# Attention into a gated feed-forward on one core: the last 64 tokens laid on both halves of the partitions, contiguous weight halves, shorter warm-up products and another written-out order

## The chip, the cores and the metric

The kernel runs on one core of one Trainium2 chip. The metric is the device time of one execution in microseconds. Three executions of the kernel before are known, and one more that the hardware profiler recorded.

## The reference

For each of 8 batches and 8 heads, 576 tokens with head size 64 are condensed into 32 memories, then read back; the heads' outputs go through a two-layer network (4608 tokens, 512 to 2048 to 512):

```python
a = softmax(phi, axis=2)                       # over the 32 memories
k_m = einsum('bhsm,bhsd->bhmd', a, k); v_m = einsum('bhsm,bhsd->bhmd', a, v)
attn = softmax(q @ k_m.T / sqrt(64))           # [576, 32] per head
x = concat_heads(attn @ v_m)                   # [4608, 512]
h = x @ w_in;  g = h * clip(h + 3, 0, 6) / 6;  out = g @ w_out
```

## The kernel before, in words

The host reorders the inputs; everything else runs on the core, in fp32 precision: each large product is made of three fp32r products (high by high, low by high, high by low).

**Weights.** w_in is loaded in 8 units of two halves (`load_w1`, L176), w_out in 8 units (`load_w2`, L181). A unit is taken apart into high and low words and rounded: ScalarE (ACT) runs `magnitude` (L189) and `rounding` (L193), VectorE (DVE) `clamp` (L197), `shift` (L200), `sign` (L205) and `total` (L214); a w_out unit is then split into a high part on ACT (L221) and a low part on GpSimd (POOL, `split_low`, L225). A finished w_in unit is also written to memory (L217) and fetched back for later batches.

**Attention of one batch.** phi comes with memories on partitions (`ptile`, L247). `maxima` (L275) reduces it, `exp_phi` (L294) takes the exponential; for batches 0 and 1 TensorE (PE) turns it into token rows (`phi_turn` L313, `phi_rows` L320), for later batches a second copy with token rows is loaded (`pnat`) and `less_max` (L325) and `phi_exp` (L329) work on it. `memories` (L337) is the sum over tokens, five token tiles per batch: four of 128 tokens and one of 64 (`S - 4 * P`). Each tile is 8 products (one per head, each two instructions) into four 32-column strips of the array. Then `weights` (L348, L349), `normalise` (L354), `turn` (L359), `turned` (L363), `scores` (L370, products of 64 rows by 32 columns on both row halves), `scores_turn` (L381), `reduce` (L392), `centre` (L396), `exponent` (L399), `invert` (L403, L404), `divide` (L408), `back` (L412), `back_high` (L416), `back_low` (L421). `fold` (L435) multiplies the condensed values into w_in, so that the network's first product runs on the 32 memories per head: its result `both` is copied by `folded_high` (L446) and `folded_low` (L450).

**Network.** Work is cut into 128 slots (batch, block of 128 hidden features). In each, `gemm1` (word `g`, L466: 12 products of 288 columns) fills `ph`; `relu` (`u`, L479, ACT), `gate` (`m`, L482, DVE), `gate_rest` (`k`, L486, ACT), `high` (`h`, L490, ACT), `low` (`l`, L493, DVE) prepare `parts`; `gemm2` (`a`, L502: 12 products of 512 columns) adds four token tiles into four PSUM banks. The last 64 tokens of two batches share one tile (`Rest`, L558). `ph`, `pk`, `turns`, `pq`, `psc` and `pv` take turns in two PSUM buffers of two banks each.

**Order.** The order on every engine is written out by hand in the string ORDER: its words are played once, each issues its instructions, and each engine runs its own in that order and waits for what they need. All loads go through one queue, SP's, in the order of their words; `load_kv` (L253) takes buffers from a ring of five that w_in units 2 to 7 share, so a load waits there until its buffer is free, and the loads behind it wait too. `warm` (`wm.N`, L588) multiplies zeros by the identity into an idle bank; ORDER holds 14 of them, most in the first 50 us, `wm.7` and `wm.9` between the slots.

The words of the attention are `mx` L275, `xp` L294, `tr` L313, `pc` L320, `xa` L325, `xe` L329, `kvm` L337, `nr` L348 and L349, `nk` L354, `tp` L359, `tk` L363, `sc` L370, `ct` L381, `cm` and `ds` L392, `cs` L396, `ex` L399, `dr` L403 and L404, `dm` L408, `bt` L412, `bh` L416, `bl` L421, `fo` L435, `vh` L446, `vl` L450; of the weights `raw`, `raw2`, `ab`, `ro`, `cl`, `sh`, `si`, `to`, `sx` and `sy` in the order above, with a first number 0 for w_in and 1 for w_out. `kvm.0.4` is batch 0's fifth token tile.

Of the kernel before, what the change touches and what calls it, by code (L numbers as in the profile page):

```python
# [64 lines left out]
a.6.1 e.0.3 m.8 fo.1.3 eo.0.0 a.6.2 vh.1.3 cl.1.4 eo.0.1 h.7 h.8 si.0.4 vl.1.3 l.7 a.6.3 raw.5.0 l.8 u.9 to.0.4 m.9
g.10 a.7 h.9 k.8 raw.5.1 g.11 si.1.3 k.9 l.9 to.1.3 ab.0.5 a.8 cl.0.5 sh.1.4 u.10 m.10 ab.1.5 u.11 g.12 m.11 k.11
xa.2.2 h.10 cl.1.5 si.1.4 k.10 a.9 to.1.4 l.10 u.12 ro.0.5 sh.0.5 m.12 fo.0.3 si.0.5 a.10 h.11 g.13 h.12 l.11 raw.6.1
vh.0.3 k.12 to.0.5 sx.3 sh.1.5 a.11 u.13 l.12 m.13 fo.1.4.5 ab.0.6 vl.0.3 si.1.5 vh.1.5 sy.3 wk.3 vl.1.5 fo.0.4.5
vh.1.4 vl.1.4 raw.7.0 a.12 raw.7.1 cl.0.6 g.14 vh.0.4 h.13 wk.4 l.13 ab.0.7 a.13.0 sx.4 sh.0.6 vh.0.5 u.14 si.0.6
# [5 lines left out]
vh.1.6 g.22 si.1.7 vl.1.7 sy.6 xe.2.2 vl.1.6 h.21 l.21 kv.2.1 u.22 a.20 g.23 to.1.7 m.22 a.21 sx.7 k.22 eo.1.1 sy.7
k.20 h.22 g.24 u.23 l.22 u.24 m.23 h.23 a.22 m.24 wk.5 kv.2.3 k.23 l.23 kv.2.2 g.25 a.23.0 g.26 h.24 u.25 wk.6
fetch.2.1 e.2.0 a.23.1 wm.7 a.23.2 m.25 k.24 xe.2.0 l.24 u.26 m.26 h.26 g.27 a.23.3 kvm.2.0 kvm.2.1 kvm.2.2 kvm.2.3
kvm.2.4 a.24.0 k.25 e.2.2 a.24.1 h.25 k.26 nr.2 kv.3.3 nk.2 l.25 g.28 u.27 e.2.1 l.26 a.24.2 m.27 e.2.3 eo.2.1 g.29
u.28 m.28 h.27 a.24.3 tp.2 fetch.2.0 rc.3.0 h.28 a.25 k.28 tk.2 l.28 u.29 eo.2.0 k.27 l.27 m.29 k.29 g.30 a.26 u.30
# [5 lines left out]
ra.0.2 h.32 kv.3.0 k.33 h.33 g.35 rl.0.3 xe.3.1 l.32 a.32.0 u.34 m.34 e.3.3 xe.3.0 l.33 g.36 u.36 h.34 eo.3.1 m.36
l.34 a.32.1 k.34 u.35 ra.0.3 fetch.2.7 eo.3.0 re.0.0 m.35 re.0.1 kvm.3.0 kvm.3.1 kvm.3.2 kvm.3.3 kvm.3.4 h.35 ro2.0
g.37 h.36 a.32.2 l.35 nr.3 nk.3 kv.4.4 l.36 k.36 u.37 k.35 g.38 m.37 h.37 u.38 a.32.3 g.39 k.37 l.37 m.38 u.39 tp.3
h.38 m.39 tk.3 a.33 fo.2.4.5.6.7 vh.2.4 vh.2.5 l.38 vh.2.6 vh.2.7 vl.2.4 a.34 k.39 h.39 vl.2.5 g.40 fetch.3.2 l.39
k.38 u.40 kv.4.0 q.3.1 m.40 a.35 k.40 vl.2.7 g.41 fetch.3.3 u.41 m.41 vl.2.6 h.40 a.36 l.40 g.42 h.41 a.37 k.41 g.43
# [588 lines left out]
```

## Time and profile before

| what | us |
|---|---|
| median of three runs (lowest, highest) | 715.05 (714.21, 715.69) |
| the profiled execution: its own time | 716.04 |
| its span, first to last instruction | 714.3 |
| PE busy in the span | 691.0 |
| DVE, ACT, POOL busy | 386.8, 325.4, 79.7 |

The span is what the trace shows; 1.7 us of the profiled execution's own time lie outside it. A "busy" PE may run at either of two clock levels, which the row PEclk of the page tells by slices of the span.

### The profile page before, as it was taken

The page shows a single profiled execution, that of the slowest core. Times are in us where ns is not written, and L with a number is a line of the kernel's source. Part 1 is how long each engine was busy: PE and PEld are TensorE (multiplying, and loading weights), DVE is VectorE, ACT ScalarE, POOL GpSimd, SP SyncE. Part 2 cuts the span into 40 slices and gives each one's busy share as a digit, 9 for nine tenths or more (in the row PEclk, how much of TensorE's full clock was granted, in tenths as well). Part 3 has the DMA queues.
Part 4 walks back from the last instruction along what each step waited for, and adds up shares of the span by engine and source line. Part 5 has one row for each costly group of instructions (what it writes and reads, how often), then busy time and mean ns, then how long its engine had stood idle before and what let it go on. Part 6 is the DMA issues. An engine that isn't in the chain of part 4 may idle for free.

```text
span 714.3 us, 12530 instructions
## 1 busy us (share of the span) xinstructions
PE 691.0 (97%) x5248; PEld 576.1 (81%) x5248; DVE 386.8 (54%) x592; ACT 325.4 (46%) x635; POOL 79.7 (11%) x59
## 2 busy tenths in 40 slices
...
PEclk8589999999999999999999999999999999999999
...
GB/s 335 325 302 403 255 123 106 46 265 78 200 233 118 248 31 61 95 201 218 24 102 102 107 182 33 215 116 240 1 71 257 3 133 1 148 60 1 1 1 73
DMA packets 28247, 98.47 MB, mean 138 GB/s; under 512 B 3104, under 2 KB 3872, under 8 KB 27168
## 3 DMA queue, kind: packets, MB, share of 16 engines
...
q8 instruction: 41, 0.67, 0.4%
q14 instruction: 14, 0.11, 0.1%
...
## 4 chain that ended last, share of the span: by engine, by line
PE 88%; DVE 5%; DMA 4%; ACT 1%; issue 0%; SPq 0%; POOL 0%; POOLq 0%; DVEq 0%; ACTq 0%
PE acc L502 46%; PE ph L466 28%; PE acc L558 6%; PE pv L435 4%; PE pk L337 3%; DMA kvt<-in_kv 2%; DMA ptile<-in_pt 1%; PE psc L370 1%; DMA nmxb<-nmx 1%; DVE sm L392 1%; DVE tmp L197 1%; DMA nmx<-nmxT 1%; DVE mx L392 1%; DVE both L450 0%; DVE st L381 0%; DVE gf L482 0%
## 5 line engine op out<-in xcount | busy, mean ns | idle before, releaser
L502 PE MATMUL acc<-w,parts 128*128 128x512 f32 x1536 | 380.9, 394 | 0.0
L502 PEld LDWEIGHTS acc<-w,parts 128*128 128x128 f32 x1536 | 279.3, 188 | 63.9 <-issue 10.3
L482 DVE SCALAR_TENSOR_TENSOR gf<-gf,ph 128x576 f32<-128x576 f32 x128 | 95.6, 752 | 185.2 <-ACT gf L479 184.8
L466 PE MATMUL ph<-phi,both 128*128 128x288 f32 x1024 | 178.4, 296 | 3.5 <-DVE gf L482 1.7
L479 ACT ACTIVATE gf<-ph,three 128x576 f32<-128x576 f32 x128 | 94.7, 742 | 187.0 <-PE ph L466 159.7
L466 PEld LDWEIGHTS ph<-phi,both 128*128 128x128 f32 x1024 | 154.8, 188 | 16.1 <-DVE both L450 3.1
L493 DVE TENSOR_TENSOR parts<-gf,parts 128x512 fp32r<-128x512 f32 x128 | 91.3, 720 | 35.7 <-ACT parts L490 35.2
L466 PE MATMUL ph<-plo,both 128*128 128x288 f32 x512 | 109.0, 294 | 0.0
L490 ACT CAST parts<-gf 128x512 fp32r<-128x512 f32 x128 | 78.8, 619 | 49.7 <-DVE gf L482 21.6
L466 PEld LDWEIGHTS ph<-plo,both 128*128 128x128 f32 x512 | 82.8, 189 | 0.0
L396 POOL TENSOR_TENSOR st<-st,mx 128x576 f32<-128x576 f32 x15 | 18.6, 1252 | 412.2 <-DVE mx L392 412.2
L450 DVE TENSOR_TENSOR both<-pv,both 128x512 fp32r<-128x512 f32 x64 | 42.1, 680 | 27.0 <-ACT both L446 26.9
L446 ACT CAST both<-pv 128x512 fp32r<-128x512 f32 x64 | 35.6, 589 | 36.8 <-PE pv L435 32.4
L558 PE MATMUL acc<-w,parts 128*128 128x512 f32 x192 | 46.3, 391 | 0.0
L558 PEld LDWEIGHTS acc<-w,parts 128*128 128x128 f32 x192 | 35.6, 188 | 8.0 <-ACT o L524 0.9
L486 ACT COPY rest<-gf 128x64 f32<-128x64 f32 x128 | 30.0, 243 | 16.1 <-DVE gf L482 16.1
L435 PE MATMUL pv<-w,kvT 64*32 64x256 f32 x1024 | 33.4, 388 | 0.4 <-DVE st L381 0.4
L225 POOL TENSOR_TENSOR w<-tmp,w 128x1024 fp32r<-128x1024 f32 x8 | 20.3, 2533 | 90.2 <-ACT w L221 90.2
L435 PEld LDWEIGHTS pv<-w,kvT 64*32 64x32 f32 x1024 | 17.7, 107 | 13.3 <-issue 3.0
L337 PE MATMUL pk<-kvt,pnat 128*32 128x129 f32 (+1 forms) x640 | 24.8, 308 | 2.9 <-DMA kvt<-in_kv 2.4
L337 PEld LDWEIGHTS pk<-kvt,pnat 128*32 128x32 f32 (+1 forms) x640 | 18.9, 122 | 9.4 <-DMA kvt<-in_kv 4.2
L421 POOL TENSOR_TENSOR plo<-pT,phi 128x576 fp32r<-128x576 f32 x15 | 22.3, 1497 | 9.7 <-ACT phi L416 9.5
...
## 6 DMA issues: line engine op xcount, KB each, us to landing
...
```

The costliest lines, as they stand in the source:

```text
L337: nc.tensor.matmul(self.pk[j * M : (j + 1) * M, g, :KV], self.pnat[:rows, t, g * P + j * M : g * P + (j + 1) * M], kvt[:rows, g * NJ + j, ...
L435: nc.tensor.matmul(self.pv[u][j * M : (j + 1) * M, g], self.kvT[rows, g, j * M : (j + 1) * M], chunk[rows, j, :].bitcast(F32), start=True, ...
L446: nc.scalar.copy(both[:, 0], self.pv[u])
L450: nc.vector.tensor_tensor(both[:, 1], self.pv[u], both[:, 0].bitcast(F32), ALU.subtract)
L466: nc.tensor.matmul(self.ph[:, hf], w[:, g, fs], x[:, g * HALF : (g + 1) * HALF], start=(i == 0), stop=(i == len(seq) - 1),)
L479: nc.scalar.activation(self.halves(), self.ph, AF.Relu, bias=three)
L482: nc.vector.scalar_tensor_tensor(self.halves(), self.halves(), 6.0, self.ph, ALU.min, ALU.mult)
L486: nc.scalar.copy(rest[:, self.f, at : at + REST], self.gf[:, MAIN:])
L490: nc.scalar.copy(self.parts[:, 0], self.gf[:, :MAIN])
L493: nc.vector.tensor_tensor(self.parts[:, 1], self.gf[:, :MAIN], self.parts[:, 0].bitcast(F32), ALU.subtract)
L502: nc.tensor.matmul(accs[self.run, t], self.parts[:, k, t * P : (t + 1) * P], w, start=self.first and i == 0, stop=self.last and i == 2,)
L558: nc.tensor.matmul(accs["rest", self.p], self.parts[:, i // 2, t * P : (t + 1) * P], w2_parts(4 * self.r + t)[i % 2], start=self.r == 0 an ...
```

## The change: what it does

- `load_kv`: the 64 tokens of the fifth tile came as 64 partitions of 4128 bytes (8 heads); now group 0's four heads lie on partitions 0 to 63 and group 1's on 64 to 127, 2064 bytes each. `memories` takes its rows from the half of the group, so that the 8 products of the fifth tile stand on two row halves of the array. phi (`ptile`, `pnat`) follows: the last 64 tokens of both groups lie side by side, one turn of 128 by 128 takes the place of two of 128 by 64 (`phi_turn`), `phi_exp`, `phi_rows` work on 128 by 128 where they had 256 columns, and `less_max` becomes two instructions on 64 partitions by 128 columns.
- Weights: each half of a w_in unit, and each w_out unit, is contiguous in memory.
- `warm`: 128 columns where there were 256; 60 of them where there were 14, all ahead of slot 0.
- Homes: `both` lies 64 bytes further, in a tile 256 bytes wider; `rs` is 64 bytes wider, so that what follows it in memory moves.
- ORDER is written anew from end to end; all other words are the same ones.

```diff
 def load_kv(b, t):
-        rows = P if t < NT - 1 else S - (NT - 1) * P
-        kvt = sb.tile([P, ROW], F32, name="kvt", **KV_RING)[:, : H * KV].rearrange("p (h x) -> p h x", h=H)
-        nc.sync.dma_start(out=kvt[:rows], in_=kv[b, t, :rows])
+        heads = H if t < NT - 1 else NJ
+        kvt = sb.tile([P, ROW], F32, name="kvt", **KV_RING)[:, : heads * KV].rearrange("p (h x) -> p h x", h=heads)
+        nc.sync.dma_start(out=kvt, in_=kv[b, t] if t < NT - 1 else kl[b])
 def memories(self, t):
             for g in range(NG):
+                rows = slice(g * REST, (g + 1) * REST) if last else slice(0, P)
                 for j in range(NJ):
+                    at = t * NG * P + (0 if last else g * P) + j * M
                     nc.tensor.matmul(
                         self.pk[j * M : (j + 1) * M, g, :KV],
-                        self.pnat[:rows, t, g * P + j * M : g * P + (j + 1) * M],
-                        kvt[:rows, g * NJ + j, :],
+                        self.pnat[rows, at : at + M],
+                        kvt[rows, j if last else g * NJ + j, :],
-                        tile_position=(0, j * M),
+                        tile_position=(g * REST if last else 0, j * M),
 def less_max(self, k):
...
+            for g in range(NG):
+                rows = slice(g * REST, (g + 1) * REST)
+                nc.vector.tensor_tensor(part[rows], part[rows], self.nmx[rows, g * P : (g + 1) * P], ALU.add)
 def load_w1(u, k):
-        nc.sync.dma_start(out=part, in_=w1[u, :, k * n : (k + 1) * n])
+        nc.sync.dma_start(out=part, in_=w1[u, k])
 def load_w2(u):
-        nc.sync.dma_start(out=part, in_=w2[:, u])
+        nc.sync.dma_start(out=part, in_=w2[u])
 def weights(self):
-            self.rs = sb.tile([P, ALIGN], F32, name="rs", tag="rs", bufs=1)[:, :NG].unsqueeze(2)
+            self.rs = sb.tile([P, ALIGN + SHIFT], F32, name="rs", tag="rs", bufs=1)[:, :NG].unsqueeze(2)
 def folded_high(self, u):
-            both = vw[self.b, u] = sb.tile([P, 2, NG, UC], F32R, name="both", **VW_RING)
+            both = sb.tile([P, UNIT + ALIGN], F32R, name="both", **VW_RING)[:, SHIFT : SHIFT + UNIT]
+            both = vw[self.b, u] = both.rearrange("p (k g f) -> p k g f", k=2, g=NG)
 def warm(_):
-        nc.tensor.matmul(idle[:, :UC], ident, rest[:, :2].rearrange("p f s -> p (f s)"), start=True, stop=True)
+        nc.tensor.matmul(idle[:, :P], ident, rest[:, 0], start=True, stop=True)
 ORDER (its beginning)
-wm.1 pt.0 wm.5 raw.0.1 raw.0.0 wm.2 pt.1 wm.8 raw2.0 wm.6 raw.1.1 wm.3 raw.1.0 wm.12 kv.0.2 kv.0.0 mx.0 kv.0.1 xp.0.2
-xp.0.1 tr.0.2 wm.11 ab.0.0 kv.0.3 xp.0.0 cl.0.0 kv.0.4 ro.0.0 tr.0.0 mx.1 tr.0.1 sh.0.0 xp.1.1 si.0.0 xp.1.0 q.0.1
-ab.1.0 to.0.0 q.0.0 pc.0.0 pc.0.2 pc.0.1 cl.1.0 raw2.1 xp.1.2 sh.1.0 tr.1.0 ab.0.1 si.1.0 tr.1.1 ro.1.0 cl.0.1 sh.0.1
-ro.0.1 kvm.0.0 to.1.0 pc.1.0 kv.1.0 kvm.0.1 si.0.1 sx.0 kvm.0.2 kv.1.2 sy.0 kvm.0.3 kv.1.1 kvm.0.4 kv.1.3 wm.0 nr.0
-kv.1.4 nk.0 q.1.0 to.0.1 tp.0 tk.0 pc.1.1 sc.0.1 sc.0.0 ct.0.1 cm.0.1 fo.0.1 ct.0.0 vh.0.1 cs.0.1 ab.1.1 cm.0.0 fo.0.0
-cs.0.0 ex.0.1 wm.13 cl.1.1 vh.0.0 ds.0.1 ex.0.0 ro.1.1 sh.1.1 dr.0.1 vl.0.0 dm.0.1 ds.0.0 tr.1.2 kvm.1.0 dr.0.0 bt.0.1
-kvm.1.1 raw.2.0 dm.0.0 kvm.1.2 raw.2.1 bh.0.1 q.1.1 kvm.1.3 bt.0.0 pc.1.2 bl.0.1 raw2.2 kvm.1.4 vl.0.1 raw.3.0 bh.0.0
-wm.10 pt.2 nr.1 bl.0.0 nk.1 raw2.5 raw2.3 si.1.1 tp.1 g.0 raw.4.1 tk.1 to.1.1 ab.0.2 raw.6.0 sc.1.0 u.0 wm.4 cl.0.2
-ro.0.2 m.0 ct.1.0 g.1 h.0 sh.0.2 l.0 sc.1.1 cm.1.0 u.1 a.0.0 ct.1.1 k.0 ab.1.2 cs.1.0 a.0.1 m.1 g.2 si.0.2 h.1 ex.1.0
-ro.1.2 cm.1.1 fo.1.1 to.0.2 a.0.2 vh.1.1 k.1 u.2 a.0.3 cs.1.1 vl.1.1 raw.3.1 wk.1 m.2 g.3 raw2.6 l.1 ex.1.1 pn.2 sx.1
-cl.1.2 raw.4.0 fo.0.2 wk.2 sh.1.2 u.3 a.1 ds.1.0 sy.1 raw2.4 h.2 dr.1.0 vh.0.2 m.3 ro.1.5 vl.0.2 ds.1.1 dm.1.0 ab.1.3
-g.4 ro.1.3 l.2 si.1.2 a.2 h.3 k.2 u.4 to.1.2 ab.0.3 dr.1.1 l.3 k.3 g.5 sx.2 dm.1.1 m.4 bt.1.0 ro.0.3 sy.2 a.3 bt.1.1
-u.5 h.4 m.5 k.4 bh.1.1 l.4 bh.1.0 fo.1.0 bl.1.1 mx.2 fo.1.2 a.4 vh.1.2 q.2.1 bl.1.0 q.2.0 vh.1.0 mo.2 vl.1.2 h.5
...
+wm.48 wm.14 pt.0 wm.30 raw2.1 wm.18 pt.1 wm.45 raw.0.0 wm.5 wm.16 raw.0.1 wm.26 wm.49 raw2.0 wm.43 wm.27 raw.1.0 wm.34
+wm.54 raw.1.1 wm.59 wm.29 wm.13 wm.19 kv.0.0 mx.0 wm.10 wm.47 wm.7 wm.44 wm.41 wm.51 wm.20 xp.0.1 wm.53 wm.55 xp.0.0
+xp.0.2 kv.0.1 tr.0.0 ab.1.1 wm.17 wm.37 wm.21 wm.31 ro.1.1 wm.38 kv.0.2 mx.1 wm.57 wm.9 wm.28 tr.0.2 wm.3 wm.0 wm.11
+cl.1.1 kv.0.3 xp.1.1 wm.42 wm.52 sh.1.1 wm.33 xp.1.0 tr.0.1 wm.58 si.1.1 ab.0.0 kv.0.4 wm.35 to.1.1 ro.0.0 cl.0.0
+pc.0.0 q.0.1 ro.1.0 sh.0.0 si.0.0 pc.0.1 pc.0.2 ab.1.0 tr.1.0 to.0.0 wm.2 tr.1.1 xp.1.2 ab.0.1 cl.1.0 wm.32 sh.1.0
+kvm.0.0 pc.1.0 si.1.0 ro.0.1 wm.36 kv.1.1 kvm.0.1 cl.0.1 q.0.0 pc.1.1 sh.0.1 kv.1.0 kvm.0.2 to.1.0 wm.25 kv.1.2
+kvm.0.3 kvm.0.4 kv.1.3 wm.24 nr.0 kv.1.4 wm.22 si.0.1 wm.56 nk.0 q.1.1 wm.46 tp.0 to.0.1 tk.0 sc.0.1 fo.0.0 ct.0.1
+wm.40 vh.0.0 cm.0.1 sc.0.0 vl.0.0 cs.0.1 ct.0.0 tr.1.2 kvm.1.0 pc.1.2 cm.0.0 ex.0.1 fo.0.1 raw.2.0 cs.0.0 kvm.1.1
+q.1.0 ds.0.1 kvm.1.2 ex.0.0 raw.2.1 dr.0.1 vh.0.1 kvm.1.3 raw.5.0 ds.0.0 wk.0 dm.0.1 kvm.1.4 raw2.2 wm.6 dr.0.0 wm.50
+nr.1 raw.3.1 wm.39 nk.1 bt.0.1 wm.12 wk.1 tp.1 dm.0.0 bh.0.1 wm.8 bt.0.0 tk.1 bl.0.1 raw2.3 sc.1.1 vl.0.1 bh.0.0 wm.23
+ct.1.1 sx.0 wm.4 raw.3.0 wm.15 wm.1 bl.0.0 sc.1.0 sy.0 g.0 ct.1.0 ab.0.2 raw2.7 cm.1.0 cm.1.1 g.1 u.0 cl.0.2 ro.0.2
+cs.1.1 m.0 g.2 u.1 cs.1.0 h.0 m.1 ex.1.1 l.0 g.3 h.1 sh.0.2 k.0 ex.1.0 l.1 u.2 a.0.0 si.0.2 sx.1 a.0.1 to.0.2 k.1 u.3
+a.0.2 ab.1.2 m.3 sy.1 a.0.3 raw.5.1 wk.2 m.2 fo.0.2 pt.2 ds.1.1 h.2 fo.1.2 q.2.0 a.1 vh.0.2 pn.2 dr.1.1 l.2 raw2.5
+ab.1.3 raw.4.0 dm.1.1 ds.1.0 k.3 ab.0.3 vl.0.2 cl.1.2 k.2 g.4 sh.1.2 vh.1.2 ro.1.2 dr.1.0 si.1.2 a.2 u.4 dm.1.0 vl.1.2
...
```

## Rows read from the trace of the kernel before

**Rows 1.** The page, part 2: the granted clock of PE in 40 slices.

```profile
PEclk8589999999999999999999999999999999999999
```

**Rows 2.** Busy us of each engine (instructions), clock, DMA share and GB/s, by stretch.

```profile
0.00:62.04 62.04, 44.28 (x409) 28.44 (x409) 44.82 (x69) 38.68 (x68) 12.97 (x14) 0.78 0.93 334
62.04:126.00 63.96, 63.96 (x455) 53.34 (x456) 59.15 (x87) 46.80 (x88) 15.18 (x8) 1.00 0.54 192
```

**Rows 3.** Waits of PE from 64 to 709: engine, line, waited for, us, times, longest.

```profile
PE ph L466 <- DVE both L450: 0.4, 1, 0.4
```

**Rows 4.** The longest waits of DVE up to 64 us; columns as in rows 3.

```profile
DVE rs L348 <- PE pk L337: 6.0, 2, 4.3
DVE tmp L197 <- ACT tmp L189: 3.5, 1, 3.5
DVE nmx L275 <- DMA ptile<-in_pt: 3.4, 1, 3.4
```

**Rows 5.** Timeline of DVE: start, us, line, operation, idle before it.

```profile
11.88 0.68 DVE L200 TENSOR_SCALAR tmp<-tmp 128x1024 uint32<-128x1024 uint32 x1
12.60 1.29 DVE L205 SCALAR_TENSOR_TENSOR tmp<-raw,tmp 128x512 uint32<-128x512 uint32 x2
13.81 1.29 DVE L214 CUSTOM_DVE_ANT_0 w<-raw,tmp 128x1024 uint16<-128x1024 uint16 x2
15.01 0.69 DVE L197 TENSOR_SCALAR tmp<-tmp 128x1024 f32<-128x1024 f32 x1
...
25.63 0.16 DVE L348 TENSOR_SCALAR rs<-pk 128x2 f32<-128x2 f32 x1 [4.25 <-PE pk L337]
...
29.23 0.78 DVE L381 STREAM_TRANSPOSE st<-psc 128x576 f32<-128x576 f32 x1 [2.05 <-PE psc L370]
...
52.45 2.25 DVE L214 CUSTOM_DVE_ANT_0 w<-raw,tmp 128x1024 uint16<-128x1024 uint16 x2
...
56.49 2.88 DVE L197 TENSOR_SCALAR tmp<-tmp 128x1024 f32<-128x1024 f32 x1
```

**Rows 6.** Timeline of PE: batch 1's `memories` and the fifth `gemm1`.

```profile
36.49 3.67 PE L337 MATMUL pk<-kvt,pnat 128*32 128x129 f32 x64
...
62.04 1.04 PE L466 MATMUL ph<-phi,both 128*128 128x288 f32 x4 [1.29 <-DVE gf L482]
```

**Rows 7.** Stretches of 1.6 us; columns as in rows 2.

```profile
17.60:19.20 1.60, 1.36 (x18) 0.59 (x16) 1.57 (x4) 1.60 (x3) 0.00 (x0) 0.50 1.09 403
19.20:20.80 1.60, 0.49 (x12) 0.39 (x12) 1.60 (x3) 1.60 (x4) 0.00 (x0) 0.50 1.05 177
20.80:22.40 1.60, 1.55 (x32) 1.00 (x23) 0.57 (x1) 0.46 (x1) 1.06 (x1) 0.50 0.98 230
...
32.00:33.60 1.60, 1.60 (x18) 0.50 (x2) 1.57 (x4) 1.60 (x3) 0.04 (x1) 0.50 1.08 184
...
36.80:38.40 1.60, 1.60 (x36) 1.47 (x32) 1.57 (x4) 0.67 (x1) 0.00 (x0) 0.50 0.14 42
```

**Rows 8.** Timeline of POOL: the first `split_low`.

```profile
21.34 2.35 POOL L225 TENSOR_TENSOR w<-tmp,w 128x1024 fp32r<-128x1024 f32 x1 [20.04 <-ACT w L221]
```

**Rows 9.** The chain that ended last, in order: start, us, what.

```profile
277.12 1.89 PE pv L435 x64
...
392.32 1.58 PE ph L466 x12
...
394.61 2.47 PE pk L337 x80
```

**Rows 10.** Timeline of PE around `wm.7`.

```profile
164.66 0.85 PE L502 MATMUL acc<-w,parts 128*128 128x512 f32 x3
165.36 0.59 PE L588 MATMUL acc<-rest,ident 128*128 128x256 f32 x2
165.60 1.05 PE L502 MATMUL acc<-w,parts 128*128 128x512 f32 x3
166.49 0.68 PE L466 MATMUL ph<-phi,both 128*128 128x288 f32 x4
```

More of the change, by code (lines that the diff above doesn't have):

```diff
@@ L65 @@
[L65 to L69, printed above, removed]
@@ L75 @@
[L75 to L79, printed above, removed]
@@ L85 @@
[L85 to L89, printed above, removed]
@@ new lines @@
+ab.1.3 raw.4.0 dm.1.1 ds.1.0 k.3 ab.0.3 vl.0.2 cl.1.2 k.2 g.4 sh.1.2 vh.1.2 ro.1.2 dr.1.0 si.1.2 a.2 u.4 dm.1.0 vl.1.2
+h.3 fetch.2.2 m.4 ro.1.3 to.1.2 k.4 h.4 g.5 l.3 sx.2 l.4 bt.1.1 sy.2 a.3 u.5 bt.1.0 ro.1.7 m.5 bh.1.1 mx.2 bh.1.0
+bl.1.1 fo.1.1 fo.1.0 vh.1.1 mo.2 a.4 vh.1.0 bl.1.0 vl.1.1 raw2.4 h.5 vl.1.0 ab.1.5 l.5 k.5 cl.1.3 sp.2 ro.1.5 q.2.1
+g.6 cl.0.3 raw2.6 ro.0.3 sh.0.3 sh.1.3 a.5.0 u.6 si.0.3 g.7 ro.0.5 m.6 si.1.3 k.6 a.5.1 h.6 u.7 g.8 l.6 e.0.0 m.7
+a.5.2 to.0.3 u.8 a.5.3 e.0.1 m.8 eo.0.0 a.6.0 h.7 e.0.3 raw.4.1 ro.1.4 g.9 to.1.3 e.0.2 cl.1.5 k.7 eo.0.1 k.8 a.6.1
```

235 lines of the change are left out of this document (126 added, 109 removed).

## The prediction

> **What bounds the kernel now.** I read the stages first. Up to 62.04 us, where the fifth `gemm1` (`g.4`) begins, PE is busy 44.28 us at a mean clock of 0.78; in the next 63.96 us it is never idle [rows 2], and between 64 and 709 us it waits 0.4 us in all [rows 3]. So from slot 4 on the time is PE's own work, at full clock [rows 1]; nothing that another engine does there is worth anything, and what is left to gain is the start and the number and size of PE's products. Then I asked what holds the start. `g.4` waits 1.29 us for `gate` on DVE [rows 6], and DVE is busy 44.82 of the 62.04 us [rows 2], so the start is a queue of DVE work with holes of 17.2 us in it. The holes: 3.4 us for the first phi, 3.5 for the first weights, 6.0 in two waits for `memories` (4.25 ahead of `nr.0`, so 1.75 ahead of `nr.1`) [rows 4, 5], 2.05 ahead of `ct.0.1` [rows 5]. Behind them stand the loads: DMA moves 403 GB/s, and 177 and 230 while the 64-row tile `kv.0.4` is under way, 184 for `kv.1.4` [rows 7].
>
> **The start.** I compare DVE's work ahead of `g.4` in the two orders. Before, DVE must reach `m.3`; after, `vl.0.2`, which frees the PSUM buffer. Both lists have 54 words; they differ in four (`dr.1.0 vl.1.1 cl.1.2 sh.1.2` against `vl.0.2 ds.1.1 dr.1.1 l.2`), a reciprocal pair, a `vl` and two operations of 0.7 us on either side. PE's products ahead of `g.4` differ only in which unit is folded. So `g.4` moves by what DVE's holes shrink or grow.
>
> *Hole for the second phi.* `raw2.1` now comes ahead of `pt.1` in place of `raw.0`'s two halves, the same bytes, so I let `pt.1` land as before. DVE has no `cl.0.0` (0.69 [rows 5]) to do while it waits: 3.5 + 0.69 = 4.2 us where 3.5 were, 0.7 worse. Contiguous rows may make it land sooner; the floor is no wait.
>
> *Hole ahead of `nr.0`.* After `mx.1`, at about 11.9 us, the new order holds `cl`, `sh`, `si`, `to` of `raw2.1` and `raw.0`, then `cl sh si` of `raw2.0`, `cl.0.1 sh.0.1`, `to.1.0`. From start to start one `sh` takes 0.72, `si` 1.21, `to` 1.20, `cl` about 0.7 [rows 5]; four `cl`, four `sh`, three `si`, three `to` are 2.8 + 2.9 + 3.6 + 3.6 = 12.9, so DVE works until 24.8. `kvm.0.4`, which ends the wait, comes with its load. Ahead of that load's end stand 1.05 MB more than before (`raw2.1`), 2.6 us at 403 GB/s [rows 7]. The half-partition load cost (2 x 403 - 177 - 230) x 1.6 / 403 = 1.6 us [rows 7]; on 128 partitions I let it go at the common rate. So 2.6 - 1.6 = 1.0 later, less some 0.4 for fewer rounds in PE (below): `nr.0` at 26.2 against 25.63, and a hole of 1.4 against 4.25. The bound on the other side: the load is as slow on 128 partitions, and `nr.0` comes at 27.8.
>
> The Trainium skill, SBUF — State Buffer, section "Door 1: The DMA port swizzle (why [64,N] ≈ [32,N])", says that partitions 0 to 63 reach only half of the 16 DMA ports and measures 196 against 328 GB/s. By it, as an estimate, 264 KB would gain 0.5 us and not 1.6, and the gain below would be 1.1 us smaller; the trace's rates (half, over two stretches) bear the larger figure, so I keep it.
>
> *Hole ahead of `ct.0.1`.* It came 3.6 us after `nr.0` [rows 5], so at 29.8; `nr.0`, `si.0.1` and `to.0.1` fill 0.35 + 2.4 of them: 0.85 against 2.05.
>
> *Hole ahead of `nr.1`.* Ahead of it stand `ct.0.1 cm.0.1 vl.0.0 ct.0.0 cm.0.0 cs.0.0 ds.0.1 dr.0.1 ds.0.0 dr.0.0`, eight of 0.7 and two of 0.45, 6.5 us, so 36.3. The same bytes as before lie ahead of `kv.1.4`; the queue had run dry by 36.8 to 38.4 (42 GB/s [rows 7]), and two half-partition loads give back 3.2, so it lands by about 35 and `kvm.1.4` is done: hole 0 against 1.75. `vl.0.0` stands early, so batch 1's `pk` gets its buffer some 4 us sooner, and `raw.2.0`, which waits for a kv buffer, is issued before the queue runs dry.
>
> *The small holes*, 17.2 less 3.4 and the 11.55 just named, are 2.3 us in all. I keep them, with one new among them: `m.1` waits for `u.1` behind `ro.0.2` on ACT.
>
> Before: 3.5 + 4.25 + 2.05 + 1.75 = 11.55. After: 4.2 + 1.4 + 0.85 + 0 = 6.45. **Start: 5.1 us sooner.** Bounds: DVE also lost 2.2 us in one `cl` (2.88 against 0.69) and 1.0 in a pair of `to` (2.25 against 1.29) [rows 5], both beside work on POOL; should that go, 8.3. With the loads no faster 1.6 and, at `nr.1`, about 0.7 go: 2.8. `sy.0` (2.35 us [rows 8]) ran in the hole ahead of `nr.0` and now runs behind `sx.0`, about 40 us, where DVE is dense: if `cl.0.2` waits as the long `cl` did, another 2.2 go: 0.6.
>
> **Zeros.** One `wm` of 256 columns costs PE 0.43 us at full clock: from 165.36 to 166.49 is 1.13, three products of 512 alone 0.70 [rows 10]. `wm.7` and `wm.9` no longer stand between the slots: **0.9 us**. One of 128 columns is 0.22 at full and 0.43 at half clock; 26 stand ahead of the first `tr`, where PE waits for phi, 34 behind it, 14.6 us at half clock against 17.8 us of idle PE [rows 2]. Where they cover nothing they delay: four ahead of `tp.0` and four of `tp.1` may each cost 0.6. This is in the bounds, with -0.6 in place of 0.6.
>
> **Fifth tile.** `memories` is 80 instructions in 2.47 us, four strips at a time: 20 rounds of 0.12. The fold, on 64 rows by 32 columns, does 64 of twice the columns in 1.89 [rows 9], which is eight rounds of eight at 0.24: both row halves at once. So the last 16 take two rounds in place of four: 0.25 a batch, six batches behind slot 4, **1.5 us** (0 if the halves don't overlap). Two `less_max` on 64 partitions for one, `phi_exp` on half the columns and one `tr` for two lie on DVE, ACT and an idle PE: nothing, while DVE keeps up.
>
> **Homes.** Twelve products of `gemm1` take 1.58 us [rows 9], and the 128 such sets read `both` at six homes; I take 0, and 0.01 a set, 1.3 us, to either side.
>
> **Sum.** 716.04 - 5.1 - 1.5 - 0.9 = 708.5 for the profiled execution; it stood 1.0 above the median, so **707.5** for the median. What a measurement tells from no change is about 0.2%, 1.4 us.
>
> **Rivals.**
>
> *The loads hold it.* The fifth tile is no faster and the 1.05 MB counts in full: the start gives 2.8 and not 5.1: 715.05 - 2.8 - 2.4 = 709.9. For it: DMA's share is 0.93 all through the start [rows 2]. Chance 0.16.
>
> *The port.* `sy.0` meets `cl.0.2` on the memory port that the long `cl` seems to have waited for, 2.2 us [rows 5], and the start gives 2.9: 709.8. Against it: `cl.0.2` may come after its end. Chance 0.10. The Trainium skill, SBUF — State Buffer, section "SBUF: two separate sides", calls the port pair that DVE and GpSimd share an exclusive lock, the loser blocked for a whole instruction; the `cl` of 2.88 us, four times its like, agrees.
>
> *Given back.* Behind slot 4 DVE is busy 59.15 of 63.96 us [rows 2]. If the new order makes PE wait there for DVE by the start's 5.1 us, only 2.4 remain: 712.7. Against it: as much DVE work is done at `g.4` as before. Chance 0.12.
>
> *The clock, and slower.* From 17.6 to 38.4 us every stretch shows the granted clock at 0.50, 1.2 of 2.4 GHz, also where PE was busy 1.60 of 1.60 us [rows 7]; full clock is back only behind 3.67 us of dense products on 128 rows [rows 6, 1]. The new order cuts these apart (`fo.0.1` between `kvm.1.0` and `kvm.1.1`) and leans on zeros. If these fail, `g.0` to `g.3` run at half clock, 4 x 1.58, and `a.0` and `a.1` add 2 x 2.8 (four times 0.70 each [rows 10]): 11.9 - 7.5 = 4.4 slower, 719.5. It decides from where it costs 7.5, that is, if the clock is still low in `a.0`. Against it: the first slice stands at 8 tenths [rows 1], so zeros alone had raised it. Chance 0.14.
>
> **Chances.** The forecast, from 704.5 to 709, has 0.48. Faster: 0.48 + 0.16 + 0.10 + 0.03 of those given back = 0.77; same: 0.09 of those and 0.02 of the clock's = 0.11; slower 0.12. The range reaches from 703 (start 8.3, `pt.1` sooner by 1.5) to 715, where the clock's case begins.
>
> **What would show it.** DVE's wait ahead of `nr.0` near 1.4, none ahead of `nr.1`, `g.4` at about 57; no stretch at 200 GB/s at the fifth tiles; the 80 instructions of `memories` in 2.2 us; PE without waits behind `g.4`. Wrong it would be with PEclk at 0.5 beyond 45 us, a `cl.0.2` of over 2 us, or PE waits for DVE between 60 and 130 us.

## The result, and the profile after

| | before | after |
|---|---|---|
| median (lowest, highest), us | 714.63 (713.28, 715.69), 4 runs | 707.25 (706.76, 708.52), 4 runs |
| span of the profiled execution | 714.3 | 705.5 |
| `g.4` begins, slot 64, slot 112 | 62.04, 376.00, 624.57 | 56.14, 368.60, 616.02 |

The ratio is 0.9896, 95% interval 0.9875 to 0.9916: faster, by 7.4 us. Of the span's 8.8 us, 5.9 are won up to `g.4` and 2.9 behind it. Line numbers of after are a little higher: `total` is L217, `memories` L348, `weights` L359, `fold` L446, `gemm1` L478, `gate` L494, `gemm2` L514, `split_low` L228.

DVE's timeline of after, which answers to [rows 5] (last column: idle before, and what ended it):

```profile
8.65 1.35 DVE L279 TENSOR_REDUCE nmx<-ptile 128x2 f32<-128x1152 f32 x1 [2.56 <-DMA ptile<-in_pt]
...
23.87 0.16 DVE L359 TENSOR_SCALAR rs<-pk 128x2 f32<-128x2 f32 x1 [0.98 <-PE pk L348]
...
26.62 0.78 DVE L392 STREAM_TRANSPOSE st<-psc 128x576 f32<-128x576 f32 x1
...
33.78 0.10 DVE L359 TENSOR_SCALAR rs<-pk 128x2 f32<-128x2 f32 x1
...
40.58 0.68 DVE L200 TENSOR_SCALAR tmp<-tmp 128x1024 f32<-128x1024 f32 x1
...
46.28 3.47 DVE L217 CUSTOM_DVE_ANT_0 w<-raw,tmp 128x1024 uint16<-128x1024 uint16 x2
49.67 1.41 DVE L494 SCALAR_TENSOR_TENSOR gf<-gf,ph 128x576 f32<-128x576 f32 x2
...
53.37 0.68 DVE L462 TENSOR_TENSOR both<-pv,both 128x512 fp32r<-128x512 f32 x1
```

The four holes that the prediction added up (4.2, 1.4, 0.85 and 0) are 2.56, 0.98, 0 and 0. But `to.0.2` at 46.28 takes 3.47 us where a pair took 1.29 [rows 5]. POOL's timeline shows what ran beside it, `sy.1` (`sy.0`, at 37.94, ends before `cl.0.2`). I call it a meeting when operations of DVE and POOL run side by side and one of them takes far longer than alone:

```profile
37.94 2.44 POOL L228 TENSOR_TENSOR w<-tmp,w 128x1024 fp32r<-128x1024 f32 x1 [0.99 <-ACT w L224]
...
46.55 2.65 POOL L228 TENSOR_TENSOR w<-tmp,w 128x1024 fp32r<-128x1024 f32 x1 [3.15 <-ACT w L224]
```

And PE's timeline, for `a.0`, two folds, `a.1` and `g.4`, shows what that cost:

```profile
45.21 2.93 PE L514 MATMUL acc<-w,parts 128*128 128x512 f32 x12
50.47 1.58 PE L446 MATMUL pv<-w,kvT 64*32 64x256 f32 x32 [2.33 <-DVE gf L494]
51.98 4.33 PE L514 MATMUL acc<-w,parts 128*128 128x512 f32 x12
56.14 0.68 PE L478 MATMUL ph<-phi,both 128*128 128x288 f32 x4
```

PE waits 2.33 us for `gate`, which stands behind `to.0.2` on DVE, and twelve products like those that took 2.93 then take 4.33. `vl.0.2`, the last line of DVE above, ends at 54.05; `g.4`, which the prediction let wait for it, comes 2.1 us later, behind `a.1`. By stretch (columns as in [rows 2], the clock third from the end) DMA moves 414 and 415 GB/s while `kv.0.4` lands and 321 at `kv.1.4`, where [rows 7] had 177 and 230, and 184; the clock is full all through, but for the stretch behind PE's wait, where it falls to 0.50:

```profile
20.80:22.40 1.60, 1.05 (x18) 0.68 (x18) 1.56 (x3) 0.64 (x2) 0.00 (x0) 1.00 1.05 414
22.40:24.00 1.60, 1.35 (x35) 0.87 (x35) 0.62 (x2) 0.00 (x0) 0.00 (x0) 1.00 1.03 415
...
30.40:32.00 1.60, 1.60 (x56) 1.12 (x56) 1.53 (x4) 1.17 (x3) 0.00 (x0) 1.00 1.02 321
...
52.00:54.00 2.00, 2.00 (x9) 1.61 (x6) 2.00 (x5) 2.00 (x5) 1.41 (x1) 0.50 1.04 422
54.00:56.00 2.00, 2.00 (x9) 1.59 (x8) 1.93 (x6) 2.00 (x4) 0.09 (x1) 0.79 1.01 407
...
62.00:126.00 64.00, 62.76 (x453) 52.63 (x452) 58.55 (x86) 49.23 (x87) 12.61 (x6) 1.00 0.49 169
```

Behind 62 us PE, which waited 0.4 us there before [rows 3], now waits 2.9 us in all:

```profile
PE ph L478 <- DVE both L462: 1.2, 4, 0.5
PE pv L446 <- DMA w<-w_kept: 0.9, 1, 0.9
PE ph L478 <- DVE gf L494: 0.8, 1, 0.8
```

The 96 instructions of the fifth tile in the six batches behind the start keep PE busy 2.7 us, where before it was 3.9 (line, shape, count, busy us and mean ns):

```profile
L348 PE MATMUL pk<-kvt,pnat 64*32 64x129 f32 x96 | 2.7, 282 | 0.0
```

One more difference was in no step of the prediction. From start to start, by place in the twelve and as a median over the slots between 130 and 640 us, `gemm2`'s first four products took 235, 231, 232, 231 ns before and 226, 227, 227, 227 after.

### The profile page after: what moved, and what is told of

It is laid out like the page before. It is cut to its first block, busy times and chain, and to the rows that moved or that the text cites. A ratio compares the mean times of both kernels' runs of the same rounds, so it can differ in the third digit from the quotient of the medians.

```text
span 705.5 us, 12734 instructions
## 1 busy us (share of the span) xinstructions
PE 687.3 (97%) x5338; PEld 581.0 (82%) x5338; DVE 384.2 (54%) x598; ACT 325.3 (46%) x635; POOL 79.6 (11%) x59
## 5 line engine op out<-in xcount | busy, mean ns | idle before, releaser
L514 PE MATMUL acc<-w,parts 128*128 128x512 f32 x1536 | 378.9, 393 | 0.0
L514 PEld LDWEIGHTS acc<-w,parts 128*128 128x128 f32 x1536 | 280.8, 189 | 61.4 <-issue 6.5
L494 DVE SCALAR_TENSOR_TENSOR gf<-gf,ph 128x576 f32<-128x576 f32 x128 | 95.5, 752 | 177.2 <-ACT gf L491 177.0
L478 PE MATMUL ph<-phi,both 128*128 128x288 f32 x1024 | 175.9, 294 | 2.4 <-DVE both L462 1.2
L478 PEld LDWEIGHTS ph<-phi,both 128*128 128x128 f32 x1024 | 154.6, 188 | 14.4 <-issue 3.0
L505 DVE TENSOR_TENSOR parts<-gf,parts 128x512 fp32r<-128x512 f32 x128 | 87.6, 692 | 41.1 <-ACT parts L502 40.5
L478 PE MATMUL ph<-plo,both 128*128 128x288 f32 x512 | 109.9, 296 | 0.0
L478 PEld LDWEIGHTS ph<-plo,both 128*128 128x128 f32 x512 | 81.6, 188 | 0.1
L446 PE MATMUL pv<-w,kvT 64*32 64x256 f32 x1024 | 32.7, 382 | 3.3 <-DVE gf L494 2.3
L446 PEld LDWEIGHTS pv<-w,kvT 64*32 64x32 f32 x1024 | 17.9, 106 | 15.2 <-DVE gf L494 3.9
L228 POOL TENSOR_TENSOR w<-tmp,w 128x1024 fp32r<-128x1024 f32 x8 | 19.7, 2464 | 77.0 <-ACT w L224 77.0
L410 ACT ACTIVATE st<-st 128x576 f32<-128x576 f32 x16 | 10.9, 685 | 25.9 <-POOL st L407 25.5
L348 PE MATMUL pk<-kvt,pnat 128*32 128x129 f32 (+1 forms) x640 | 19.9, 277 | 2.0 <-DMA kvt<-in_kv 1.9
```

Source lines behind the costliest of these rows:

```text
L446: nc.tensor.matmul(self.pv[u][j * M : (j + 1) * M, g], self.kvT[rows, g, j * M : (j + 1) * M], chunk[rows, j, :].bitcast(F32), start=True, ...
L478: nc.tensor.matmul(self.ph[:, hf], w[:, g, fs], x[:, g * HALF : (g + 1) * HALF], start=(i == 0), stop=(i == len(seq) - 1),)
L494: nc.vector.scalar_tensor_tensor(self.halves(), self.halves(), 6.0, self.ph, ALU.min, ALU.mult)
L505: nc.vector.tensor_tensor(self.parts[:, 1], self.gf[:, :MAIN], self.parts[:, 0].bitcast(F32), ALU.subtract)
L514: nc.tensor.matmul(accs[self.run, t], self.parts[:, k, t * P : (t + 1) * P], w, start=self.first and i == 0, stop=self.last and i == 2,)
```

## Experiments

Ratios are to the kernel before, run on the same chip in the same rounds (its medians there 715.62, 714.53 and 714.64 us). The changed kernel itself, run again, gives 0.9899.

### What the loads are worth

**The old fifth tile** (64 rows by 8 heads, 16 products in four strips) in the changed kernel:

```diff
-        nc.sync.dma_start(out=kvt, in_=kv[b, t] if t < NT - 1 else kl[b])
+        nc.sync.dma_start(out=kvt[:rows], in_=kv[b, t, :rows])
-            tile_position=(g * REST if last else 0, j * M),
+            tile_position=(0, j * M),
... (and the layout of phi and of the rows that goes with it)
```

> The changed kernel with the old form of the last 64 tokens: 64 rows by 8 heads in one load, phi's two transposes, 16 products in four strips. The prediction's two steps together (theory): each of the two loads 1.6 us later, a hole of some 2.5 us ahead of `nr.0` in place of 0.98, and four rounds in place of two in each of eight batches, 1.2 behind the start: 707.25 + 1.6 + 0.4 + 1.2 = 710.5. If the load on half the partitions is hidden (rival): only the rounds, 708.5, with the wait ahead of `nr.0` still near 1 us.

Measured 712.13 us (708.45 to 713.23), ratio 0.9941 [0.9918, 0.9963]. `kv.0.4` lands at 24.88 us where after has 23.27: the load is worth 1.61, and the hole ahead of `nr.0` is 3.19 in place of 0.98. The first theory holds (the ratio is 3 us above that of the changed kernel run again), with a surprise in the profiled execution, the lowest of six, 708.45: `g.0` begins 3.6 us later than after's, `g.4` 0.14 earlier. DVE, then POOL:

```profile
26.08 0.16 DVE L351 TENSOR_SCALAR rs<-pk 128x2 f32<-128x2 f32 x1 [3.19 <-PE pk L340]
...
49.88 1.29 DVE L217 CUSTOM_DVE_ANT_0 w<-raw,tmp 128x1024 uint16<-128x1024 uint16 x2
```

```profile
50.15 3.27 POOL L228 TENSOR_TENSOR w<-tmp,w 128x1024 fp32r<-128x1024 f32 x1 [3.16 <-ACT w L224]
```

`sy.1` begins 0.27 us behind `to.0.2`, as in after, but here it is POOL that waits (3.27 against some 2.4) and DVE that goes through. Who wins is not fixed by the order of the words.

**Weights in pieces of rows**, as before, in the changed kernel:

```diff
-        nc.sync.dma_start(out=part, in_=w1[u, k])
+        nc.sync.dma_start(out=part, in_=w1[u, :, k * n : (k + 1) * n])
-        nc.sync.dma_start(out=part, in_=w2[u])
+        nc.sync.dma_start(out=part, in_=w2[:, u])
... (and the host's arrays)
```

> The changed kernel with the weights' halves as before, pieces of rows of a larger array in place of contiguous blocks. If contiguous halves made the second phi land sooner (theory; it landed at 8.53 us and before at 10.49, behind as many bytes): `pt.1` lands at 9.5 to 10.5, DVE's wait for it is 3.5 to 4.5 us in place of 2.56, and the time is 1 to 2 us more, 708.5 to 709. If the new order of the first loads alone did that (rival): the wait stays at 2.6 and the time at 707.3.

Ratio 0.9903 [0.9886, 0.9920], 707.74 us: no difference that can be measured. For the second phi and the time the rival was right: the wait is 2.81 us, nearly as after. But further on, which neither guess looked at, `kv.0.4` lands at 24.37, 1.10 later than in after, and `nr.0` comes at 25.32, 1.45 later (PE's clock stood at 0.50 from 22 to 24 us, in after at 1.00, so not all of the 1.45 need be the load's). Contiguous weights do speed the loads; `g.4` begins at 56.08 all the same, because PE's clock did not fall behind its wait in this execution:

```profile
51.93 1.33 PE L446 MATMUL pv<-w,kvT 64*32 64x256 f32 x32 [2.33 <-DVE gf L494]
53.19 3.06 PE L514 MATMUL acc<-w,parts 128*128 128x512 f32 x12
```

### What the order and the zeros are worth

**The old order**, with its 14 products of zeros of 256 columns, all else as after:

```diff
 ORDER (its beginning)
-wm.48 wm.14 pt.0 wm.30 raw2.1 wm.18 pt.1 wm.45 raw.0.0 wm.5 wm.16 raw.0.1 ...
+wm.1 pt.0 wm.5 raw.0.1 raw.0.0 wm.2 pt.1 wm.8 raw2.0 wm.6 raw.1.1 wm.3 ...
-        nc.tensor.matmul(idle[:, :P], ident, rest[:, 0], start=True, stop=True)
+        nc.tensor.matmul(idle[:, :UC], ident, rest[:, :2].rearrange("p f s -> p (f s)"), start=True, stop=True)
```

> The order of before, with its 14 products of zeros of 256 columns, on the changed loads, fifth tile, weights and homes. If loads and homes carry the gain (theory): the wait ahead of `nr.0` falls from 4.25 us to about 2.5 and that ahead of `nr.1` from 1.75 to 0, so the start is 3.4 us sooner, the fifth tile is worth 1.2 behind it and the homes 3.5 to 4: 706 to 706.5, so the new order with its zeros is worth nothing net. If the order carries the pitch and the most of the start (rival): 3.4 and 1.2 alone, 710.

706.18 us, ratio 0.9866 [0.9847, 0.9885]: at the least not slower than after. The time is the first theory's. `nr.0` comes at 20.75, behind a wait of 0.45 where I expected 2.5 (before 4.25 [rows 5]), `nr.1` behind 1.54; `g.4` at 56.90. In DVE's and PE's timelines:

```profile
20.75 0.16 DVE L356 TENSOR_SCALAR rs<-pk 128x2 f32<-128x2 f32 x1 [0.45 <-PE pk L345]
...
51.35 2.89 DVE L197 TENSOR_SCALAR tmp<-tmp 128x1024 f32<-128x1024 f32 x1
```

```profile
56.90 1.04 PE L475 MATMUL ph<-phi,both 128*128 128x288 f32 x4 [1.28 <-DVE gf L491]
```

The first theory had the wait ahead of `nr.0` too long, since it counted the tile alone: `kv.0.4` lands at 20.15 us, 4.28 sooner than before, of which the tile's form is worth some 1.6, and the second phi at 9.29 where it was 10.48. The rest is the contiguous weights'. So the changed loads and homes alone bring `g.4` 5.14 us forward. The new order is worth 0.8 more there, which it gives back: behind 62 us the old one has one wait of 0.6 where the new one has 2.9.

**No zeros at all** (60 words taken out of ORDER):

```diff
-wm.48 wm.14 pt.0 wm.30 raw2.1 wm.18 pt.1 ...
+pt.0 raw2.1 pt.1 ...
```

> The changed kernel without any of its 60 products of zeros (their output is read by nobody). If the zeros hold TensorE's clock up (theory, the prediction's rival on the clock): the granted clock is 0.5 from some point of the start until the dense products, `g.0` to `g.3` take up to twice their 0.79 us a half and `a.0`, `a.1` up to twice 2.8: 5 to 11 us later, 712 to 718. If the true products alone keep the clock, the zeros only stand in PE's way (rival): the same to 1 us faster, 706 to 707.

706.42 us, ratio 0.9868 [0.9849, 0.9886]: not slower than with them. The clock is lower in two stretches of the start,

```profile
24.00:36.00 12.00, 8.27 (x164) 3.40 (x163) 11.19 (x21) 4.89 (x11) 3.41 (x3) 0.80 1.02 382
36.00:46.00 10.00, 9.98 (x73) 8.59 (x66) 7.67 (x13) 7.75 (x14) 5.84 (x4) 0.73 1.00 406
```

but `g.4` begins only 0.65 us later. The time is the rival's, and the mechanism in part the theory's: in these two profiles the zeros hold the clock, and a lower clock there costs little. They don't hold it always: in the profile of the changed kernel run again, zeros and all, it falls to 0.56 between 22 and 24 us and to 0.59 between 36 and 40. And something speaks for leaving them out: without them `kv.0.4` lands at 22.05 us, 1.22 sooner than in after, and `nr.0` comes without a wait. The other pair of runs below shows the same (22.03 against 23.15); why, no run shows.

### The meeting on the memory

**The changed kernel again**, for its spread:

> The changed kernel unaltered, for the same chip as the other three: 707 to 708.5 (0.9896 of before). If `to.0.2` meets `sy.1` in every execution its runs lie within 1 us of each other; if the meeting turns on a tenth of a microsecond (the run with the old fifth tile missed it by 0.27 us in its profile and had runs from 708.4 to 713.2), some lie 3 us lower.

707.80 us (703.95 to 708.82), ratio 0.9899 [0.9877, 0.9921]; one of six runs lies 2.6 us below the next. In its profile (span 706.9) `to.0.2` met `sy.1`, and before that `bl.0.0`, 0.71 us alone, met `sy.0`:

```profile
38.94 2.92 DVE L432 TENSOR_TENSOR plo<-pT,phi 128x576 fp32r<-128x576 f32 x1
...
49.61 3.47 DVE L217 CUSTOM_DVE_ANT_0 w<-raw,tmp 128x1024 uint16<-128x1024 uint16 x2
```

My expectation said of the run with the old fifth tile that it missed the meeting; its rows above show that it met and won.

**`sy` earlier**:

```diff
-... tk.0 sc.0.1 fo.0.0 ct.0.1 wm.40 vh.0.0 cm.0.1 sc.0.0 vl.0.0 cs.0.1 ct.0.0 ... sx.0 ... sy.0 ... sx.1 ... sy.1
+... tk.0 sc.0.1 fo.0.0 ct.0.1 wm.40 vh.0.0 sx.0 cm.0.1 sc.0.0 vl.0.0 cs.0.1 sy.0 ct.0.0 ... sx.1 ... sy.1
```

> The changed kernel with four words moved: `sx.0` behind `vh.0.0` and `sy.0` behind `cs.0.1` (POOL is idle there from 29.4 to 32.4 us), and `sx.1 sy.1` at the old places of `sx.0 sy.0`, so that no `sy` runs beside `to.0.2`. If the meeting of `sy.1` and `to.0.2` on the memory costs the start its 2.2 us and, through PE's idle time of 2.33 us and the clock that falls behind it, another 1.4 to 1.6 (theory): `to.0.2` takes 1.28 us in place of 3.47, `a.1` 2.8 in place of 4.33, `g.4` begins at 52.5 us in place of 56.1, and the time is 703.5 to 704. If something else ends last there, the loads or POOL (rival): `g.4` at 55 or later, 706 to 707.3.

706.67 us, ratio 0.9889 [0.9874, 0.9903]; `g.4` at 55.92. `to.0.2` takes 1.29, as expected, but the moved `sy.0` meets another operation, `cs.0.0`, alone 0.76. DVE, then POOL:

```profile
30.99 2.08 DVE L406 TENSOR_TENSOR st<-st,mx 128x576 f32<-128x576 f32 x1
```

```profile
30.08 2.38 POOL L227 TENSOR_TENSOR w<-tmp,w 128x1024 fp32r<-128x1024 f32 x1
```

The meeting was moved, not removed. `cs.0.0` stands ahead of `nr.1` on DVE, which comes at 35.80 in place of 33.78, and `g.0` begins 3.1 us later than in after.

**`sy.1` later**, by one word:

```diff
-... si.0.2 sx.1 a.0.1 to.0.2 k.1 u.3 a.0.2 ab.1.2 m.3 sy.1 ...
+... si.0.2 a.0.1 to.0.2 k.1 u.3 a.0.2 ab.1.2 sx.1 m.3 sy.1 ...
```

> The changed kernel with one word moved: `sx.1` behind `u.3` and `ab.1.2` on ACT, so that `sy.1`, which waits for it, begins at 48.4 us, after `to.0.2`, and runs beside `m.3 m.2 ds.1.1`, of which none was slowed beside POOL so far; `l.2` and the small add of `dr.1.1` may wait for its end at 51. If the meeting with `to.0.2` is what the start loses (theory): `to.0.2` 1.28 us, PE's wait of 2.33 us gone, no clock drop, `g.4` at 52.5 to 53 and 704 us on this scale (before at 714.5 to 715.6). If behind slot 4 DVE can't follow (the prediction's rival, given back): `g.4` as soon, but PE's waits behind it grow from 2.9 us to 5 or more, and the time is 706 to 707.

706.18 us (704.48 to 707.80), ratio 0.9869 [0.9848, 0.9890]; the profiled execution, one of 704.48, spans 702.7. DVE, POOL, PE, and PE's waits behind 36 us:

```profile
46.17 1.28 DVE L216 CUSTOM_DVE_ANT_0 w<-raw,tmp 128x1024 uint16<-128x1024 uint16 x2
47.37 1.41 DVE L493 SCALAR_TENSOR_TENSOR gf<-gf,ph 128x576 f32<-128x576 f32 x2
48.70 0.75 DVE L402 TENSOR_REDUCE sm<-st 128x18 f32<-128x576 f32 x1
49.48 1.33 DVE L413 TENSOR_SCALAR sm<-sm 128x18 f32<-128x18 f32 x1
```

```profile
48.38 2.40 POOL L227 TENSOR_TENSOR w<-tmp,w 128x1024 fp32r<-128x1024 f32 x1 [5.09 <-ACT w L223]
```

```profile
49.43 3.04 PE L513 MATMUL acc<-w,parts 128*128 128x512 f32 x12
52.96 0.79 PE L477 MATMUL ph<-phi,both 128*128 128x288 f32 x4 [0.49 <-DVE both L461]
```

```profile
PE ph L477 <- DVE both L461: 1.7, 5, 0.5
PE ph L477 <- DVE gf L493: 1.1, 2, 0.8
PE pv L445 <- DMA w<-w_kept: 0.7, 1, 0.7
```

This is the theory's picture: `to.0.2` at its own length, no wait of 2.33 us, `a.1` at full clock, `g.4` 3.18 us sooner, and of these 2.81 are still there at the last slot. Only a small add, 0.18 alone, now waits out `sy.1` (1.33). The rival, given back, takes 0.4. The timed runs stand only some 2 us below after's, where the theory had 3, on intervals that overlap. The mean granted clock of each execution tells a part of the rest: the two at 704.5 us have 1.000 and 0.999, the three longer ones 0.994 to 0.998, so in these the clock fell somewhere. That after often misses its meeting is not borne out: in all eight traced executions with `sy.1` at after's place (after's, the same kernel again, the old fifth tile, the weights in rows, no zeros, and three with old homes) it begins beside `to.0.2`. DVE lost in seven of them, POOL in one, and behind the seven waits of PE, of 2.29 to 2.44 us, the clock fell in five. How these cases are spread over the executions without a trace is not known.

**That, and no zeros**:

```diff
-... si.0.2 sx.1 a.0.1 ... ab.1.2 m.3 sy.1 ...   (and 60 words wm.N)
+... si.0.2 a.0.1 ... ab.1.2 sx.1 m.3 sy.1 ...
```

> The run with `sx.1` later, and without the 60 products of zeros (nobody reads their output). If the zeros are worth a clock step where PE idles in the start (theory, from the run without zeros alone: `g.4` 0.65 us later): `g.4` some 0.6 to 1 us later than in the run with them, 704.6 to 705. If they are worth nothing or stand in the way (rival): the same within 0.3 us, or sooner.

705.14 us, ratio 0.9860 [0.9843, 0.9877]. In the profile `g.4` comes 0.71 later than with the zeros (53.67), as the theory says; in the timed runs nothing is lost. In two pairs, then, the zeros gain 0.7 us at `g.4` in a profile and no time that can be measured.

### The homes

Four combinations of old and new homes, all else as after:

```diff
-            both = sb.tile([P, UNIT + ALIGN], F32R, name="both", **VW_RING)[:, SHIFT : SHIFT + UNIT]
-            both = vw[self.b, u] = both.rearrange("p (k g f) -> p k g f", k=2, g=NG)
+            both = vw[self.b, u] = sb.tile([P, 2, NG, UC], F32R, name="both", **VW_RING)
-            self.rs = sb.tile([P, ALIGN + SHIFT], F32, name="rs", tag="rs", bufs=1)[:, :NG].unsqueeze(2)
+            self.rs = sb.tile([P, ALIGN], F32, name="rs", tag="rs", bufs=1)[:, :NG].unsqueeze(2)
```

Both edits:

> The changed kernel with the old homes of `both` and `rs` (no 64 columns more, no shift of 16), everything else as after (707.25). If the homes set the pitch of the products (theory): the first four products of each `gemm2` go back from 227 ns to 231 to 235 and `gemm1` loses some 10 ns a slot, together 3.5 to 4 us over 128 slots: about 711, with the start unchanged (the fifth `gemm1` at 56.1 us). If the new order sets the pitch and the homes are worth nothing, as the prediction had it (rival): 707.3 and a pitch of 227 ns.

Only the second:

> The changed kernel with the old home of `rs` (64 columns, so all tiles behind it lie 64 bytes lower), and the new one of `both`. If `both`'s own 64 bytes set the pitch of `gemm1` alone and the tiles behind `rs` that of `gemm2` (theory): `gemm1` as after (126 and 128 ns at its second and third product), `gemm2`'s first four products back at 231 to 235 ns, 2 us slower than after. If `both` sets the two (rival): all as after, 707.3; if the tiles behind `rs` set the two: 2.5 to 3 slower.

Only the first:

> The changed kernel with the old home and size of `both`, and the new one of `rs`, the fourth of four combinations. With the two old the products lost 1.45 ns each in `gemm2` and 0.65 in `gemm1`, with `rs` alone old more. If the distance between `both` and the tiles that are read with it decides (theory): as bad as the other mixed one, a last slot 4 us later than after's, 711. If the home of the tiles behind `rs` decides alone (rival): as after, 707.3, with 227 ns at `gemm2`'s first products.

Start to start in ns (medians as above), and how much later than after's the last slot begins, counted from `g.4`:

| `both`, `rs` | `gemm2`, products 1 to 4 | `gemm1`, 2, 3, 10 | last slot, us | time, ratio |
|---|---|---|---|---|
| new, new (after) | 226, 227, 227, 227 | 126, 128, 131 | 0 | 707.80, 0.9899 |
| old, old | 235, 231, 232, 231 | 133, 132, 140 | 2.5 | 710.29, 0.9918 [0.9898, 0.9938] |
| new, old | 233, 236, 226, 231 | 132, 132, 132 | 4.1 | 711.01, 0.9946 [0.9926, 0.9966] |
| old, new | 237, 233, 236, 225 | 140, 132, 132 | 5.4 | 714.96 (one run) |

The old order on the new homes shows after's pitch (226, 227, 227, 227), so the order has no part in it. Neither home decides alone: the two mixed ones are the worst. The pitch and the last slot are read from one trace each. In the timed runs the two old homes cost 1.4 us, by ratios whose intervals (0.9898 to 0.9938, and 0.9877 to 0.9921 for the changed kernel again) still overlap; with only `rs` old it is 3.4, clear of the noise. That is against what I expected of the run with the old `rs` (`both`'s own home leaves `gemm1` as slow as the old one), and with the first theory of the last run, by more than it said. In the last row's one run `g.4` also comes 2.1 us later than in after, which is in its time and not in the column before it.

### A version that beats both

The old order on the changed loads and homes, two words moved behind `l.2` and the two products of zeros between the slots left out:

```diff
-... pn.2 sx.1 cl.1.2 raw.4.0 fo.0.2 wk.2 sh.1.2 u.3 ... g.4 ro.1.3 l.2 si.1.2 a.2 ...  wm.7 ... wm.9
+... pn.2 sx.1 raw.4.0 fo.0.2 wk.2 u.3 ... g.4 ro.1.3 l.2 cl.1.2 sh.1.2 si.1.2 a.2 ...
```

> The old order on the changed loads and homes, with `cl.1.2 sh.1.2` moved behind `l.2`, so that no `cl` of 2.89 us stands ahead of `m.3`, for which PE waits 1.28 us, and without `wm.7` and `wm.9`, 0.43 us each between the slots. If these are what that order loses (theory): `g.4` at 55.6 us in place of 56.9 and 0.86 us less behind it, 704 to 704.4 where the old order alone gave 706.2. If another operation takes the `cl`'s place beside `sy.1`, or `si.1.2` comes too late behind it (rival): 705 to 706.

703.13 us (702.10 to 703.52), ratio 0.9828 [0.9810, 0.9846]: 4.9 us under the changed kernel by the ratios, on intervals that don't touch, and below the 704 of the theory. In place of the `cl` of 2.89, the small add waits for `sy.1`, and `g.4` no longer waits for `gate`:

```profile
51.75 1.60 DVE L411 TENSOR_SCALAR sm<-sm 128x18 f32<-128x18 f32 x1
```

```profile
55.11 0.68 PE L475 MATMUL ph<-phi,both 128*128 128x288 f32 x4
```

## Why the prediction was right

The number was right, 707.5 for 707.25, and so was the mechanism at large: a start shorter by its loads, and fewer products behind it. Its parts were off in both directions, and that the errors cancelled so closely is luck. Between the two profiled executions 8.8 us were won where the parts add up to 7.5; the median agrees to 0.25 because the one before stood 1.0 above its median and that of after stands at its own.

- **Half-partition load: right.** 1.6 us was the price; 1.61 is what `kv.0.4` lands sooner than in the run with the old form, and 2.2 at `nr.0`, with the rounds, where 2.0 were counted (the clock stood at 0.50 there in that run from 24.0 to 25.6 us, and at 1.00 in after). By the two rates that the Trainium skill, SBUF — State Buffer, section "Door 1: The DMA port swizzle (why [64,N] ≈ [32,N])", measures for half and for all partitions, the prediction had 0.5 as an estimate; the run bears three times that.
- **Contiguous weights: priced at nothing.** The prediction let `pt.1` land as before and the loads behind it go at the old rate. They are worth 1.1 us at `kv.0.4` and up to 1.45 at `nr.0`. The second phi is another matter: it lands 1.95 us sooner with a w_out unit ahead of it, and 1.84 with that unit in pieces (the wait is 2.56 and 2.81), where the prediction had let it land as before. With the two, DVE's holes fell from 11.55 to 3.5 us and not to 6.45.
- **The port: right in kind, wrong in place.** `sy.0` did not meet `cl.0.2`; `sy.1` met `to.0.2`, 2.2 us, and with PE's idle time and the clock behind it the meeting cost 3.2 at `g.4`, which the profile of the run with `sy.1` later shows. This pair stood in no rival, and its cost is about the 2.9 that the two gains left out above had won. The Trainium skill, SBUF — State Buffer, section "Who interferes with whom", says that a DVE instruction with two inputs in SBUF contends with a GpSimd instruction that reads SBUF, and that one in a two-port mode contends with GpSimd. The rows agree in which ones were slowed: `to` (1.28 to 3.47), `bl` (0.71 to 2.92), `cs` (0.76 to 2.08), `cl` (0.69 to 2.89) and the add of `dr` (0.18 to 1.33), and not `gate`, whose second input is in PSUM, nor `reduce`. `cl` and the add have one input; in which mode they ran no row shows.
- **Start: 5.1 predicted, 5.9 measured, and its path right only as far as DVE.** Up to the word that each order needs, DVE's work is the same (44.7 and 44.5 us), and its idle time falls from 17.2 to 9.5, so `vl.0.2` ends 7.85 us sooner than `m.3` did. But `g.4`, which came 0.14 behind `m.3`, comes 2.09 behind `vl.0.2`, since PE was still in `a.1` at the low clock: 7.85 + 0.14 - 2.09 = 5.90. In the run with `sy.1` later `g.4` does wait for `vl.0.2`, 0.49 us, as the prediction had it.
- **Zeros between the slots 0.9, fifth tile 1.5**: no run takes the first out alone; the fifth tile is mis-sized: a batch's 80 instructions take 2.28 us from the first to what follows, where they took 2.47 [rows 9], so 0.19 and not 0.25 a batch, 1.2 in six.
- **Homes: the step that failed.** Taken as 0, with 1.3 to either side; they are worth 2.5 us by the trace of the run with the old ones, and some 3 without the 0.5 by which its wait for `w_kept` was shorter.
- **PE without waits behind `g.4`: failed.** It waits 2.9 us where it waited 0.4. That is the rival "given back" in part. Behind `g.4` 1.2 + 0.9 + 3.0 - 2.5 (2.9 less 0.4) = 2.6, of 2.9 measured.
- **The clock, 719.5: no.** The clock did stand at 0.50 beyond 45 us, which the prediction had named as a sign against it, but only for some 3.4 us, at a cost of 1.4 in `a.1`, not for a whole start; and without any zeros the time is not longer.

What stays open: how much of the old order's lead over the new one (2.1 us between two ratios with 0.2% to either side) is real, which tiles' distance in memory sets the pitch, and what decides who loses a meeting.
